# One buffer each for rounded q and its remainder, a 24th resident weight tile, fixed places for raw q and k, and GpSimd in order of need in the first pairs

## The chip, the cores and the metric

The kernel runs on one core of one Trainium2 chip. The metric is the device time of one execution in microseconds (us), which is a little longer than the span that the profile shows. Engines are named as in the profile: PE is TensorE, PEld its weight loads, DVE is VectorE, ACT is ScalarE, POOL is GpSimd, SP is SyncE, which here only issues transfers.

## What is computed

Causal attention for 8 batches of 12 heads (sequence 448, head size 64), and then a soft mixture of 8 experts with 4 slots each over the 3584 rows that come out:

```
scores = q @ k.T / sqrt(64), masked above the diagonal     # 96 heads, 448 x 448
attn   = softmax(scores);  x = attn @ v                    # x: 3584 x 768
logits = x @ phi                                           # 3584 x 32
d = softmax over rows of logits;   slot_input = d.T @ x    # 32 x 768
slot_out[e] = relu(slot_input[e] @ w1[e]) @ w2[e]          # w1: 768 x 1024, w2: 1024 x 768
c = softmax over slots of logits;  out = c @ slot_out      # 3584 x 768
```

## The kernel before

**Attention.** Two heads make a pair; there are 48 pairs, and `block(p)` (line 536) issues the work around pair p. Every engine runs its instructions in the order in which the program writes them (`_InOrder`, line 55). Transfers wait only for what they overwrite. Heads are numbered i = 2p and 2p + 1; the halves of a tile that hold them are h0 and h1.

Scores are exact sums of rounded parts. For each pair ACT rounds raw q into `qd` (`cast_q`, line 226) and raw k into `ks` (`cast_k`, line 230). The raw tiles hold the data twice, in partitions 0 to 63 and 64 to 127. POOL then puts the remainder of k into partitions 64 to 127 of `ks` (`sub_k`, line 234), and the remainder of q into partitions 64 to 127 of `r2` (`sub_q`, line 244). `copy_k2` (ACT, line 239) copies the rounded k beside a block of ones in `k2`. PE forms scores in two groups: `scores1` (line 250) multiplies `ks` by `qd`, and `scores2` (line 326) multiplies `k2` by `r2`. In between DVE finds maxima per row of the first group (`max_keys`, `max_row`), and POOL spreads their negatives into partitions 0 to 13 of `r2` (`max_spread`, line 315), so that `scores2` adds remainder and shift in one go. ACT takes the exponent (`exps`), and PE multiplies by v (`attv_pair`).

In block p, PE runs in this order: `scores2(2p)`, `scores1_all(2p+2)`, `scores2(2p+1)`, `scores1_all(2p+3)`, `attv_pair(p)` with a transposition of maxima in its middle, then logits work, transpositions, and on to the next block. POOL runs `sub_q(p+1)`, `sub_k(p+2)`, `max_spread(2p+2)`, `max_spread(2p+3)`. ACT runs `exps`, a copy, `exps`, `copy_k2(p+1)`, `cast_q(p+2)`, `cast_k(p+3)`. SP loads raw q for pair p+3 after `sub_q`, raw k for pair p+4 after `sub_k`, then v and in odd blocks a weight tile.

`scores1` of an even head above 4 reads two columns past its own half of `ks`, that is, the first two columns of the other head's half (`KP`, line 265).

`qd`, `ks` and `r2` have two buffers each, used by turns. Raw q and k share a pool of four buffers (line 92), and two early ones borrow room that weights take later.

**Experts.** The weights are 64 tiles of 128 x 1536 numbers (768 KB each), loaded in a fixed order by number n; six tiles per expert, w1 in four and the first half of w2 in two, then the second halves of w2. `RES` = 23 of them (n = 0 to 22) are loaded during attention into room of their own (`load_w`, line 163, called at line 542): the first 22 in pairs of tiles, the last alone in `wone`. `TW1` = 12 more (n = 23 to 34) go, one after the other, into the room that attention leaves (`wt[0]`, lines 822 to 824): each waits until the tiles that lay in its place were read for the last time. This room is taken from the raw tiles first, then `qd`, `ks`, `r2`, v and x, and the oldest tiles of the logits last. From n = 35 (which is loaded as part of a tile named `hw`) on, tiles go where a read weight tile lay, and in the resident room two at a time (1536 KB). SP issues all this in order.

The experts (`expert_in`, `expert_out`) run over e = 0 to 7; the last stage (`combine`) multiplies c by the slots' output and writes 11 MB out.

**The first pairs** have an order written out by hand (lines 505 to 531, and the cases for p == 0 in `block`). `warm` issues matmuls on no data of use; `START` and `WARM` are their numbers.

Of the kernel before, what the change touches and what calls it, by code (L numbers as in the profile page):

```python
# [9 lines left out]
F32 = mybir.dt.float32  # L10
F32R = mybir.dt.float32r
BF16 = mybir.dt.bfloat16
AF = mybir.ActivationFunctionType
# [4 lines left out]
P = 128  # L18
# [12 lines left out]
NEG = -float(2 ** 33)  # L31
NHD = 2 * NPAIR
NR, XB, XT = 2, 3, 2
RES, TW1 = 23, 12

HT = 2
WN, PAD = 1536, 168
WARM = (2, 5, 2, 3, 3)
START = (8, 3, 2)


FILL = 9
# [38 lines left out]
def attention_soft_moe(ctx: ExitStack, tc: tile.TileContext, qk, va, phi, w1, w2, out):  # L81
    nc = _Core(tc)
    const = ctx.enter_context(tc.tile_pool(name="const", bufs=1, side="left"))
    wone = ctx.enter_context(tc.tile_pool(name="wone", bufs=1, side="left"))
    wres = ctx.enter_context(tc.tile_pool(name="wres", bufs=RES // 2, side="left"))
    att, early = ExitStack(), ExitStack()

# [1 line left out]
    xtp = early.enter_context(tc.tile_pool(name="xtp", bufs=1, side="right"))  # L89
    wk = early.enter_context(tc.tile_pool(name="wk", bufs=1, side="right"))  # L90
    fix = early.enter_context(tc.tile_pool(name="fix", bufs=1, side="right"))
    raw = early.enter_context(tc.tile_pool(name="raw", bufs=4, side="right"))
    ps_1 = att.enter_context(tc.tile_pool(name="ps_1", bufs=1, space=PSUM))
    scs = ExitStack()
    ps_s = scs.enter_context(tc.tile_pool(name="ps_s", bufs=1, space=PSUM))
# [1 line left out]


    x_, va_, pt_ = [None] * XB, [None, None], [None, None]
    qd_, ks_ = [fix.tile([P, 2, S], F32R, name="qd0")], [fix.tile([P, 2 * S + KP], F32R, name="ks0")]  # L100
    r2_ = [fix.tile([P, 2, S], F32R, name="r20")]
    qd_.append(fix.tile([P, 2, S], F32R, name="qd1"))
    ks_.append(fix.tile([P, 2 * S + KP], F32R, name="ks1"))
    va_[0] = fix.tile([P, NCH, 2, VC], F32, name="va0")
    x_[1] = fix.tile([P, NCH, 3 * P], F32, name="x1")
    r_ = [fix.tile([P, RW], F32, name=f"r{i}") for i in range(2)]
    k2_ = fix.tile([P, 2 * S + KP], F32R, name="k2")
    r2_.append(fix.tile([P, 2, S], F32R, name="r21"))
    pt_[0] = wk.tile([P, 1024], F32, name="pt0")
    va_[1] = wk.tile([P, NCH, 2, VC], F32, name="va1")  # L110
    pt_[1] = wk.tile([P, 1024], F32, name="pt1")
# [10 lines left out]
    def load_qk(p, a, hs=slice(0, 2), eng=nc.sync):  # L122
        if p < NPAIR:
            if hs.start == 0:

                st["raw", a, p] = (wres.tile([P, 2 * WN], F32, tag="w", name=f"qk{a}_{p}")[:, 0:2 * S]
                                   .rearrange("p (h s) -> p h s", h=2)
                                   if (p, a) in ((1, 0), (2, 1)) else
                                   raw.tile([P, 2, S], F32, tag="qk", name=f"qk{a}_{p}"))
            eng.dma_start(out=st["raw", a, p][:, hs], in_=qk[p, :, a, hs])  # L130

    def loads_v(p, eng=nc.sync):
# [18 lines left out]
    def slot(n, name, dtype=F32):  # L151
        m = place(n)
        if m >= RES:
            return wt[0].tile([P, WN], dtype, tag=f"wa{m}", name=name)
        if m == RES - 1:
            return wone.tile([P, WN], dtype, tag="w1", name=name)
        k = (n - m, m // 2)
        if k not in twos:
            twos[k] = wres.tile([P, 2 * WN], F32, tag="w", name=name)
        t = twos[k][:, WN * (m % 2):WN * (m % 2) + WN]  # L160
        return t if dtype is F32 else t.bitcast(dtype)

    def load_w(n):
        if n < len(order):
            m, e, h, u = order[n]
            t = wtiles[order[n]] = slot(n, f"w{n}")
            src, q = (w1 if m == 0 else w2)[e, h], place(n)
            if n <= NBUF or q >= RES - 1:
                nc.sync.dma_start(out=t, in_=src[:, WN * u:WN * u + WN])
            elif u:  # L170

                nc.sync.dma_start(out=twos[n - q, q // 2], in_=src)
# [25 lines left out]
    for x in (x_[1], x_[0], x_[2]):  # L198
        nc.vector.memset(x[:, NCH - 1], 0.0)
    nc.scalar.activation(out=identb, in_=ident, func=AF.Copy)  # L200
    load_qk(1, 1, eng=nc.scalar)
    load_qk(2, 0)
    load_qk(3, 1)
    for i in range(NR):
        nc.gpsimd.memset(r2_[i][0:64, :, :].bitcast(F32), 0.0)
        nc.vector.memset(ks_[i][:, 2 * S:2 * S + KP].bitcast(F32), 0.0)
        nc.vector.memset(r_[i], -3.0e38)
    nc.vector.memset(k2_[0:64, 0:2 * S].bitcast(F32), 1.0)
# [5 lines left out]
    def warm(n, w=None, a=None):  # L214

        w = misc("warm") if w is None else w
        a, z = (identb, tri) if a is None else (a, a)
        for _ in range(n):
            nc.tensor.matmul(w, a, z.unsqueeze(1).to_broadcast([P, w.shape[1] // P, P]),
                             start=True, stop=True)  # L220
# [4 lines left out]

    def cast_q(p, hs=slice(0, 2)):
        if p < NPAIR:
            nc.scalar.activation(out=qd_[p % NR][:, hs], in_=st["raw", 0, p][:, hs], func=AF.Copy)

    def cast_k(p, hs=slice(0, 2)):  # L230
        if p < NPAIR:
            nc.scalar.activation(out=kv(p)[:, hs], in_=st["raw", 1, p][:, hs], func=AF.Copy)

    def sub_k(p, hs=slice(0, 2), eng=None):
        if p < NPAIR:
            ks = kv(p)[64:P, hs]
            (eng or nc.gpsimd).tensor_tensor(out=ks, in0=st["raw", 1, p][64:P, hs], in1=ks, op=ALU.subtract)
# [5 lines left out]

    def sub_q(p, hs=slice(0, 2), eng=None):
        if p < NPAIR:
            (eng or nc.gpsimd).tensor_tensor(out=r2_[p % NR][64:P, hs], in0=st["raw", 0, p][64:P, hs],
                                             in1=qd_[p % NR][64:P, hs], op=ALU.subtract)


    def scores1(i, part):  # L250
        if i >= NHD:
            return
        p, h = divmod(i, 2)
        ks, qd = ks_[p % NR], qd_[p % NR]
        if ("s", i) not in st:
            st["s", i] = s_[i % 3]
            st["open"] = set()
        s = st["s", i]

        bank = part in ("c12", "k1", "k2")  # L260
        start = bank not in st["open"]
        st["open"].add(bank)
        if part[0] == "k":
            c = int(part[1])
            o, w, m = S * h + P * c, S - CQ0[c], min(P, S - P * c + (KP if i > 4 or i % 2 else 0))
            nc.tensor.matmul(s[0:m, SCOL[c]:SCOL[c] + w], ks[:, o:o + m],
                             qd[:, h, CQ0[c]:S], start=start, stop=False, skip_group_check=True)
            return
        if part == "c12":
            o = s[:, SC1:SC1 + 2 * SC2].rearrange("p (a n) -> p a n", n=SC2)[:, :, 0:P]  # L270
            mask = tri.unsqueeze(1).to_broadcast([P, 2, P])
        else:
            o, mask = s[:, SC3:SC3 + AW + P], tri2
        nc.tensor.matmul(o, identb, mask, start=start, stop=False, skip_group_check=True)
# [40 lines left out]
    def max_spread(i):  # L315
        if i >= NHD:
            return
        p, h = divmod(i, 2)
        mr = st.pop(("mr", i))

        nc.gpsimd.affine_select(out=r2_[p % NR][0:NQB, h].rearrange("p (b t)->p b t", t=32),
                                in_=mr.unsqueeze(1).to_broadcast([NQB, NQB, 32]),
                                compare_op=ALU.is_equal, fill=0.0, base=0,
                                pattern=[[-1, NQB], [0, 32]], channel_multiplier=1)

    def scores2(i, cs):
        if i >= NHD:
            return
        p, h = divmod(i, 2)
        s = st["s", i]  # L330
        k2, r2 = k2_, r2_[p % NR]
        for c in cs:
            o, w, m = S * h + P * c, S - CQ0[c], min(P, S - P * c + (KP if i > 4 or i % 2 else 0))
            nc.tensor.matmul(s[0:m, SCOL[c]:SCOL[c] + w], k2[:, o:o + m],
                             r2[:, h, CQ0[c]:S], start=False, stop=True, skip_group_check=True)
# [169 lines left out]
    warm(START[0], a=x_[1][:, NCH - 1, 0:AW].bitcast(BF16))  # L505
    h0, h1 = slice(0, 1), slice(1, 2)
    cast_k(0, h0)
    cast_q(0, h0)
    copy_k2(0, h0)
    sub_k(0, h0, nc.vector)  # L510
# [8 lines left out]
    cast_k(0, h1)  # L519
    cast_q(0, h1)  # L520
    sub_k(0, h1)
    max_row(0, 0)
    max_row(0, 1)
    max_spread(0)
# [11 lines left out]
    def block(p):  # L536
        a, b = 2 * p, p // 6 - 1
        last, m6 = p == NPAIR - 1, p % 6
        if p + 1 < NPAIR:
            loads_v(p + 1, nc.sync if p + 1 < NPAIR - 1 else nc.scalar)  # L540
        if p % 2 and p // 2 < RES - 1 or p == 2 * RES - 2:
            load_w(p // 2)

        if last:
            for f in last_of:
# [5 lines left out]
        if p == 0:  # L551
            copy_k2(0, h1)
            cast_q(1, h1)
            max_row(1, 0)
            max_row(1, 1)
            max_spread(1)
            sub_k(1, h1, nc.vector)
        elif p > 1:
            xcopy(p - 2)
# [14 lines left out]
        if m6 == 2 and p > 6:  # L574
            logits_b(b)
        max_keys(a + 3, 0)
        if p:
            sub_q(p + 1)
            load_qk(p + 3, 0)
            sub_k(p + 2)  # L580
            load_qk(p + 4, 1)
        else:
            sub_q(1, h0)
            sub_k(2, h0)
        copy_k2(p + 1)
        if m6 == 2 and p > 6:
            logits_d(b, lt)
        cast_q(p + 2)
        cast_k(p + 3)
        if m6 == 3 and p > 6:  # L590
            logits_al(b)
        elif m6 == 4 and p > 6:
# [16 lines left out]
        attv_pair(p)  # L609
        max_row(a + 2, 1)  # L610
        max_spread(a + 2)
        if p == 0:
            sub_q(1, h1)
            load_qk(3, 0)
        for k in (1, 2):
            max_keys(a + 3, k)
        for k in range(2):
# [21 lines left out]
        if m6 == 2 and p > 6:  # L639
            logits_e(b, m, 1)  # L640
        max_spread(a + 3)
        if p == 0:
            sub_k(2, h1)
            load_qk(4, 1)
        if m6 in (1, 3, 5) and p > 1:
            logits_t(j, m[:, 0:P])
        for d, hf, sl, o in parts:
# [320 lines left out]
```

## Time and profile before

| | |
|---|---|
| median of 3 runs | 403.80 us (403.26 to 404.63) |
| profiled execution, its own time | 403.89 us |
| its span in the profile | 402.2 us |
| granted TensorE clock, mean | 0.984 |
| read from memory, written | 107.25 MB, 11.01 MB |

A profile row of the timeline gives start, duration, engine, operation, the tiles written and read, the shapes, and how many instructions were merged; in brackets stands idle time before it and what ended it. A row of the windows gives busy time of each engine in that stretch, the granted clock, the busy share of the 16 transfer engines and GB/s. A row of the chain of waits gives start, duration and the work that set the pace there.

### The profile page before, as it was taken

The page shows a single profiled execution, that of the slowest core. Times are in us where ns is not written, and L with a number is a line of the kernel's source. Part 1 is how long each engine was busy: PE and PEld are TensorE (multiplying, and loading weights), DVE is VectorE, ACT ScalarE, POOL GpSimd, SP SyncE. Part 2 cuts the span into 40 slices and gives each one's busy share as a digit, 9 for nine tenths or more (in the row PEclk, how much of TensorE's full clock was granted, in tenths as well). Part 3 has the DMA queues.
Part 4 walks back from the last instruction along what each step waited for, and adds up shares of the span by engine and source line. Part 5 has one row for each costly group of instructions (what it writes and reads, how often), then busy time and mean ns, then how long its engine had stood idle before and what let it go on. Part 6 is the DMA issues. An engine that isn't in the chain of part 4 may idle for free.

```text
span 402.2 us, 14066 instructions
## 1 busy us (share of the span) xinstructions
PE 368.3 (92%) x5756; PEld 295.8 (74%) x5756; DVE 293.7 (73%) x834; ACT 282.4 (70%) x395; POOL 265.3 (66%) x214
## 2 busy tenths in 40 slices
PE   6889899999999999999999999999999989997840
PEld 3678888898988898888888889888876544542420
DVE  5868788788898888898888888888975575342540
ACT  5878798898898888888888988988952112432430
POOL 5899899898898988898988989888950000000000
PEclk9999999999999999999999999999999999999985
DMA  8668877878787788777788787788679999999997
GB/s 304 230 199 282 271 266 228 245 279 278 229 286 262 244 269 289 256 240 265 262 270 259 249 272 238 274 286 257 216 279 415 420 420 423 424 418 413 398 397 339
DMA packets 34480, 119.17 MB, mean 296 GB/s; under 512 B 3824, under 2 KB 8944, under 8 KB 32880
## 3 DMA queue, kind: packets, MB, share of 16 engines
q1 hardware_dynamic: 34128, 117.55, 82.2%
q8 instruction: 45, 0.74, 0.7%
q10 hardware_dynamic: 288, 0.73, 0.5%
q14 instruction: 19, 0.16, 0.1%
HBM read 107.25 MB, written 11.01 MB: 294 GB/s over the span
## 4 chain that ended last, share of the span: by engine, by line
PE 54%; DMA 16%; POOL 12%; issue 5%; ACT 4%; DVE 4%; SPq 1%; POOLq 0%; DVEq 0%; ACTq 0%
PE s L65 28%; PE po L65 17%; DMA w<-in_w_dram 14%; POOL r L65 7%; POOL ks L65 5%; PE xm L65 3%; PE rt L65 1%; ACT ks L65 1%; PE pp L65 1%; DVE r L65 1%; DMA qk<-in_qk_dram 1%; PE hp L65 1%; ACT k L65 1%; DVE si L65 1%; PE e L65 1%
## 5 line engine op out<-in xcount | busy, mean ns | idle before, releaser
L65 DVE TRANSPOSE_TENSOR_REDUCE r<-s 128x32 f32<-128x1024 f32 x96 | 119.5, 1245 | 11.4 <-PE s L65 9.3
L65 ACT ACTIVATE pt<-s 128x1024 f32<-128x1024 f32 x96 | 98.8, 1029 | 40.6 <-PE s L65 37.8
L65 PEld LDWEIGHTS po<-va,pt 128*64 128x64 f32 x3040 | 103.6, 138 | 12.0 <-issue 11.9
L65 PE MATMUL po<-va,pt 128*64 128x65 f32 x3040 | 110.6, 224 | 0.0
L65 POOL TENSOR_TENSOR r<-qk,qd 64x896 fp32r<-64x896 f32 (+1 forms) x50 | 101.7, 2033 | 5.5 <-ACT qd L65 1.8
L65 POOL TENSOR_TENSOR ks<-qk,ks 64x896 fp32r<-64x896 f32 (+1 forms) x49 | 99.2, 2024 | 0.2
L65 PE MATMUL s<-qd,ks 128*128 128x448 f32 (+4 forms) x384 | 80.8, 322 | 0.6 <-POOL ks L65 0.4
L65 POOL TENSOR_SCALAR_AFFINE_SELECT r<-mr 14x448 fp32r<-14x448 f32 x96 | 61.5, 643 | 29.8 <-PE xm L65 18.6
L65 PE MATMUL s<-r,k 128*128 128x448 f32 (+3 forms) x384 | 65.2, 292 | 5.0 <-POOL r L65 4.3
L65 PEld LDWEIGHTS s<-r,k 128*128 128x128 f32 (+1 forms) x384 | 59.3, 176 | 11.0 <-POOL r L65 8.8
L65 PEld LDWEIGHTS s<-qd,ks 128*128 128x128 f32 (+2 forms) x384 | 52.8, 184 | 3.7 <-issue 1.4
L65 ACT ACTIVATE qd<-qk 128x896 fp32r<-128x896 f32 (+1 forms) x50 | 46.0, 920 | 1.7 <-DMA qk<-in_qk_dram 0.8
L65 ACT ACTIVATE k<-ks 64x896 fp32r<-64x896 f32 (+1 forms) x49 | 45.8, 934 | 1.2
L65 ACT ACTIVATE ks<-qk 128x896 fp32r<-128x896 f32 (+1 forms) x51 | 45.4, 892 | 1.1 <-DMA qk<-in_qk_dram 1.0
L65 PE MATMUL s<-tri,identb 128*128 128x192 bf16 x192 | 39.4, 270 | 1.1 <-DVE si L65 0.4
L65 DVE TENSOR_REDUCE r<-r 128x16 f32<-128x32 f32 x192 | 33.7, 176 | 5.0
L65 DVE TENSOR_REDUCE mr<-s 14x32 f32<-14x128 f32 x47 | 13.1, 279 | 23.1 <-ACT ks L65 12.8
L65 PE MATMUL xm<-ident,x 128*128 128x128 f32 x188 | 28.3, 273 | 0.0
L65 ACT ACTIVATE xts<-xm 128x512 f32<-128x512 f32 x47 | 27.8, 592 | 0.2 <-PE xm L65 0.2
L65 DVE TENSOR_SCALAR x<-po,sm 64x64 f32<-64x64 f32 x94 | 25.9, 276 | 0.7
L65 DVE TENSOR_TENSOR x<-po,sm 128x384 f32<-128x384 f32 (+2 forms) x49 | 25.7, 526 | 0.0
L65 DVE COPY ot<-pp 128x384 f32<-128x384 f32 x26 | 13.6, 554 | 13.4 <-PE pp L65 13.3
(138 smaller groups left out, 391.0 us busy)
## 6 DMA issues: line engine op xcount, KB each, us to landing
qk<-in_qk_dram SPq DMA_DIRECT2D x93, 448.0 KB, 4.4
w<-in_w_dram SPq DMA_DIRECT2D x43, 768.0 KB, 7.0
w<-in_w_dram SPq DMA_DIRECT2D x10, 1536.0 KB, 21.0
va<-in_va_dram SPq DMA_DIRECT2D x47, 260.0 KB, 4.6
out_dram<-ot SPq DMA_DIRECT2D x16, 384.0 KB, 6.7
out_dram<-ot SPq DMA_DIRECT2D x2, 1536.0 KB, 9.2
qk<-in_qk_dram SPq DMA_DIRECT2D x4, 224.0 KB, 3.9
hw<-in_w_dram SPq DMA_DIRECT2D x1, 768.0 KB, 8.4
```

The costliest lines, as they stand in the source:

```text
L65: return self._tc.keep_in_program_order(op(*args, **kwargs))
```

## The change

`qd` and `r2` have one buffer each. Raw q has two fixed places and raw k two, chosen by the pair's number. The 24th weight tile becomes resident, and the room that attention leaves takes 11 tiles instead of 12; the tile n = 22 is loaded in block 44 and n = 23 in block 45. In a block p above 1, POOL does `sub_k(p+2)` first and `sub_q(p+1)` second, and ACT `cast_k(p+3)` before `cast_q(p+2)`; in the blocks with p % 6 == 2 above 6, and in block 1, the second half of `sub_k(p+2)` comes after `max_spread(2p+2)`. In blocks 0 and 1 POOL's order changes, one clearing of `r2` goes, raw k of pair 1 is loaded by ACT later, and the numbers of `warm` matmuls change.

```diff
-RES, TW1 = 23, 12
+RES, TW1 = 24, 11
-START = (8, 3, 2)
+START = (9, 6, 2, 4)
...
-    raw = early.enter_context(tc.tile_pool(name="raw", bufs=4, side="right"))
...
-    qd_, ks_ = [fix.tile([P, 2, S], F32R, name="qd0")], [fix.tile([P, 2 * S + KP], F32R, name="ks0")]
-    r2_ = [fix.tile([P, 2, S], F32R, name="r20")]
-    qd_.append(fix.tile([P, 2, S], F32R, name="qd1"))
+    kraw = {n: fix.tile([P, 2, S], F32, name=f"kraw{n}") for n in (0, 1)}
+    qraw = {0: fix.tile([P, 2, S], F32, name="qraw0")}
+    ks_ = [fix.tile([P, 2 * S + KP], F32R, name="ks0")]
+    qraw[1] = fix.tile([P, 2, S], F32, name="qraw1")
+    qd = fix.tile([P, 2, S], F32R, name="qd")
     ks_.append(fix.tile([P, 2 * S + KP], F32R, name="ks1"))
...
-    r2_.append(fix.tile([P, 2, S], F32R, name="r21"))
+    r2 = fix.tile([P, 2, S], F32R, name="r2")
...
-                                   raw.tile([P, 2, S], F32, tag="qk", name=f"qk{a}_{p}"))
+                                   kraw[p % 2 if p > 1 else 1 - p] if a else qraw[p % 2 if p else 1])
...
-        if m == RES - 1:
-            return wone.tile([P, WN], dtype, tag="w1", name=name)
...
-            if n <= NBUF or q >= RES - 1:
+            if n <= NBUF or q >= RES:
...
-    load_qk(1, 1, eng=nc.scalar)
     load_qk(2, 0)
-    load_qk(3, 1)
+    nc.gpsimd.memset(r2[0:64, :, :].bitcast(F32), 0.0)
     for i in range(NR):
-        nc.gpsimd.memset(r2_[i][0:64, :, :].bitcast(F32), 0.0)
...
     cast_k(0, h0)
+    load_qk(1, 1, eng=nc.scalar)
     cast_q(0, h0)
...
-        if p % 2 and p // 2 < RES - 1 or p == 2 * RES - 2:
-            load_w(p // 2)
+        if p % 2 and p < 44 or p in (44, 45):
+            load_w(p // 2 + p // 45)
...
             cast_q(1, h1)
+            warm(START[3], pob)
...
-        if p:
+        late_k = p == 1 or m6 == 2 and p > 6
+        if p == 1:
+            sub_q(2, h0)
+            sub_k(3, h0)
+            sub_q(2, h1)
+            load_qk(4, 0)
+        elif p:
+            sub_k(p + 2, h0 if late_k else slice(0, 2))
+            if not late_k:
+                load_qk(p + 4, 1)
             sub_q(p + 1)
             load_qk(p + 3, 0)
-            sub_k(p + 2)
-            load_qk(p + 4, 1)
         else:
             sub_q(1, h0)
+            sub_q(1, h1)
+            load_qk(3, 0)
             sub_k(2, h0)
...
-        cast_q(p + 2)
-        cast_k(p + 3)
+        if p:
+            cast_k(p + 3)
+            cast_q(p + 2)
+        else:
+            cast_q(2)
+            cast_k(3)
...
         max_spread(a + 2)
-        if p == 0:
-            sub_q(1, h1)
-            load_qk(3, 0)
+        if p == 0 or late_k:
+            sub_k(p + 2, h1)
+            load_qk(p + 4, 1)
...
         max_spread(a + 3)
-        if p == 0:
-            sub_k(2, h1)
-            load_qk(4, 1)
```

More of the change, by code (lines that the diff above doesn't have):

```diff
@@ L83, in attention_soft_moe @@
     const = ctx.enter_context(tc.tile_pool(name="const", bufs=1, side="left"))
-    wone = ctx.enter_context(tc.tile_pool(name="wone", bufs=1, side="left"))
     wres = ctx.enter_context(tc.tile_pool(name="wres", bufs=RES // 2, side="left"))
@@ L227, in cast_q @@
         if p < NPAIR:
-            nc.scalar.activation(out=qd_[p % NR][:, hs], in_=st["raw", 0, p][:, hs], func=AF.Copy)
+            nc.scalar.activation(out=qd[:, hs], in_=st["raw", 0, p][:, hs], func=AF.Copy)
     def cast_k(p, hs=slice(0, 2)):
@@ L245, in sub_q @@
         if p < NPAIR:
-            (eng or nc.gpsimd).tensor_tensor(out=r2_[p % NR][64:P, hs], in0=st["raw", 0, p][64:P, hs],
-                                             in1=qd_[p % NR][64:P, hs], op=ALU.subtract)
+            (eng or nc.gpsimd).tensor_tensor(out=r2[64:P, hs], in0=st["raw", 0, p][64:P, hs],
+                                             in1=qd[64:P, hs], op=ALU.subtract)
     def scores1(i, part):
@@ L253, in scores1 @@
         p, h = divmod(i, 2)
-        ks, qd = ks_[p % NR], qd_[p % NR]
+        ks = ks_[p % NR]
         if ("s", i) not in st:
@@ L319, in max_spread @@
         mr = st.pop(("mr", i))
-        nc.gpsimd.affine_select(out=r2_[p % NR][0:NQB, h].rearrange("p (b t)->p b t", t=32),
+        nc.gpsimd.affine_select(out=r2[0:NQB, h].rearrange("p (b t)->p b t", t=32),
                                 in_=mr.unsqueeze(1).to_broadcast([NQB, NQB, 32]),
@@ L330, in scores2 @@
         s = st["s", i]
-        k2, r2 = k2_, r2_[p % NR]
+        k2 = k2_
         for c in cs:
@@ L521, in attention_soft_moe @@
     sub_k(0, h1)
+    load_qk(3, 1)
     max_row(0, 0)
```

## The prediction

> **What bounds the kernel now.** I read the page first: the share of each engine and the chain that ended last.
>
> ```profile
> PE 368.3 (92%) x5756; PEld 295.8 (74%) x5756; DVE 293.7 (73%) x834; ACT 282.4 (70%) x395; POOL 265.3 (66%) x214
> ...
> PE 54%; DMA 16%; POOL 12%; issue 5%; ACT 4%; DVE 4%; SPq 1%; POOLq 0%; DVEq 0%; ACTq 0%
> ```
>
> PE carries half the chain and transfers 16%; that is an average over two stages. The chain in order of time says where they change places, and the windows what transfers do there.
>
> ```profile
> 317.06 12.56 DMA w<-in_w_dram
> 329.68 29.73 DMA w<-in_w_dram
> 359.47 15.03 DMA w<-in_w_dram
> 374.54 0.85 PE so L65 x8
> ```
>
> ```profile
> 288.00:292.00 4.00, 4.00 (x100) 3.62 (x98) 3.53 (x9) 3.77 (x6) 3.93 (x3) 1.00 0.05 16
> 298.00:360.00 62.00, 58.05 (x817) 32.85 (x811) 33.67 (x116) 17.08 (x45) 2.28 (x9) 1.00 1.01 419
> 374.00:400.00 26.00, 10.85 (x46) 6.68 (x46) 8.69 (x18) 7.15 (x16) 0.00 (x0) 0.79 1.04 404
> ```
>
> From 317 to 374.5 weights set the time, and from 374 to 400 the output does: the transfer engines are full (share 1.01 and 1.04) from 298 on without a break. Just before, from 288 to 292, they are empty (0.05), while PE is full. So there are two prices: before 298 a microsecond counts if PE or what PE waits for loses it; after 298 only bytes count, and how early they can start. One tile is 768 KB, 0.786 MB; at 419 GB/s that is 1.87 us.
>
> **The change part by part: the end.** What moves is seen on POOL's and SP's rows in blocks 45 and 46, the last that hold subtractions.
>
> ```profile
> 287.13 2.11 POOL L65 TENSOR_TENSOR r<-qk,qd 64x896 fp32r<-64x896 f32 x1
> 289.19 2.12 POOL L65 TENSOR_TENSOR ks<-qk,ks 64x896 fp32r<-64x896 f32 x1
> 291.38 0.64 POOL L65 TENSOR_SCALAR_AFFINE_SELECT r<-mr 14x448 fp32r<-14x448 f32 x1
> 292.94 0.64 POOL L65 TENSOR_SCALAR_AFFINE_SELECT r<-mr 14x448 fp32r<-14x448 f32 x1 [0.92 <-PE xm L65]
> 293.66 2.11 POOL L65 TENSOR_TENSOR r<-qk,qd 64x896 fp32r<-64x896 f32 x1
> ```
>
> ```profile
> 295.79 0.33 SPq L65 DMA_DIRECT2D w<-in_w_dram  x1
> ```
>
> ```profile
> 310.31 0.98 SPq L65 DMA_DIRECT2D w<-in_w_dram  x2
> 313.85 0.33 SPq L65 DMA_DIRECT2D hw<-in_w_dram  x1
> ```
>
> ```profile
> hw<-in_w_dram SPq DMA_DIRECT2D x1, 768.0 KB, 8.4
> ```
>
> Before, tile 23 waits for `sub_k(47)` (done at 291.31) and tile 24 for `sub_q(47)` (293.66 + 2.11 = 295.77; issued at 295.79), since their places hold raw tiles. From there the queue holds tiles 24 to 35, twelve of them, and the last (`hw`) lands at 313.85 + 8.4 = 322.25. That is 295.79 + 12 x 1.87 = 318.2 and 4.0 more for start and completion.
>
> After, tile 23 has room of its own and is issued in block 45, into the empty stretch from 288: it costs nothing, being covered by PE's work there; without that stretch it would cost its 1.87. Counting bytes (3584 per raw place, 6144 per weight tile), tile 24 needs the two k places, tile 25 a k place, a q place and `ks0`, tile 26 the last q place. `sub_k(47)` now goes first, so tile 24 starts at about 289.3 to 290, tile 25 after `sub_q(46)`, at about 292; both land before 297. Tile 26 waits for `sub_q(47)`, which now also waits for `scores2(93)` to have read the only `r2`:
>
> ```profile
> 294.07 0.62 PE L65 MATMUL s<-r,k 128*128 128x448 f32 x4
> ```
>
> so 294.7 + 2.1 = 296.9. Then ten tiles, 26 to 35: 296.9 + 10 x 1.87 + 4.0 = 319.6, against 322.25: 2.6 us earlier. The queue must not run dry meanwhile. `hw` is gated by PE at 313.85; a tile alone takes 4.5 to land, so it can't land before 318.35.
>
> ```profile
> DMA to landing us min/median/max: 4.5/7.4/10.1
> ```
>
> 319.6 is 1.3 later, so the gate does not bind yet; 318.35 bounds the gain at 3.9. If tiles 24 and 25 gained nothing, the one resident tile would be left: 1.9. I take 2.5, a tenth off for a short gap when tile 33 (issued at 310.31) comes. All behind it, weights and output, is a full queue and moves with it. Singles fall by two and loads of two tiles rise by one, equal bytes.
>
> **Part two: the pairs.** For an ordinary pair the order on POOL turns round, but the two operations are as long as each other, so `max_spread` starts when it did. The rows of pairs 14 and 15:
>
> ```profile
> 98.87 2.11 POOL L65 TENSOR_TENSOR r<-qk,qd 64x896 fp32r<-64x896 f32 x1
> 100.93 2.10 POOL L65 TENSOR_TENSOR ks<-qk,ks 64x896 fp32r<-64x896 f32 x1
> 103.10 1.28 POOL L65 TENSOR_SCALAR_AFFINE_SELECT r<-mr 14x448 fp32r<-14x448 f32 x2
> 104.46 2.11 POOL L65 TENSOR_TENSOR r<-qk,qd 64x896 fp32r<-64x896 f32 x1
> 106.53 2.10 POOL L65 TENSOR_TENSOR ks<-qk,ks 64x896 fp32r<-64x896 f32 x1
> 108.70 0.64 POOL L65 TENSOR_SCALAR_AFFINE_SELECT r<-mr 14x448 fp32r<-14x448 f32 x1
> ```
>
> ```profile
> 105.09 0.37 PE L65 MATMUL s<-r,k 128*128 128x448 f32 x1
> ```
>
> ```profile
> 108.86 0.93 ACT L65 ACTIVATE ks<-qk 128x896 fp32r<-128x896 f32 x1
> ```
>
> New waits in pair 15: `sub_q(16)` for `scores2(31)`, which runs from 105.09 and is done by 105.8, while POOL comes to it at 106.53; and `cast_q(17)` for `sub_q(16)`, done at 108.63, while ACT comes to it at 108.86. Behind `cast_q` ACT has the next exponent and PE the next `scores1`, at 109.96 + 0.6 = 110.6; `cast_q` is done at 109.8. So these pairs cost nothing; the cover is 0.2 us on ACT and 0.8 on PE. Raw k is loaded 2 us earlier, raw q 2 us later; the transfers and SP, which waits behind neither, have that room.
>
> The seven pairs with p % 6 == 2 (8, 14, ..., 44) do cost. Before, in pair 14, the maxima were there at 102.29 + 0.24, but POOL was busy until 103.03. Now `sub_k` is cut in two halves of 1.14 (row below, 14.50), one of them behind `max_spread(30)`:
>
> ```profile
> 102.29 0.24 DVE L65 TENSOR_REDUCE mr<-rt 14x32 f32<-14x128 f32 x1
> ```
>
> ```profile
> 104.41 0.25 PE L65 MATMUL s<-qd,ks 128*66 128x64 f32 x1
> ```
>
> ```profile
> 109.96 0.45 PE L65 MATMUL s<-r,k 128*128 128x448 f32 x1
> ```
>
> `max_spread(30)` 102.57 to 103.21, second half of `sub_k` 103.28 to 104.42, `max_spread(31)` 104.5 to 105.14. PE can start pair 15 some 0.3 us sooner, but its first `scores1` reads two columns of the other head (66 in the row at 104.41), so it waits for that second half: 104.45 instead of 104.41. The gain is gone. Then `scores2(31)` at 105.17 instead of 105.09, and POOL, which ends its spreads 0.75 later, brings pair 16 to 109.96 + 0.15. PE is full afterwards and can't make it good. Bounds per pair: -0.3 (the wait goes and nothing follows) and +0.3; I take +0.15, by these rows. Seven of them: +1.05.
>
> **Part three: the first pairs.** POOL sets the pace up to pair 3.
>
> ```profile
> 13.40 1.14 POOL L65 TENSOR_TENSOR r<-qk,qd 64x448 fp32r<-64x448 f32 x1
> 14.50 1.14 POOL L65 TENSOR_TENSOR ks<-qk,ks 64x448 fp32r<-64x448 f32 x1
> 16.41 0.64 POOL L65 TENSOR_SCALAR_AFFINE_SELECT r<-mr 14x448 fp32r<-14x448 f32 x1 [0.76 <-DVE mr L65]
> ```
>
> ```profile
> 29.96 1.43 POOL L65 TENSOR_SCALAR_AFFINE_SELECT r<-mr 14x448 fp32r<-14x448 f32 x2
> ```
>
> The new order fills the 0.76 of idle time at 16.41 but cuts two more operations in halves (two times 1.14 for 2.10) and adds pauses between. Laid out from 13.40 with these durations, the spread of 29.96 starts at 29.8: -0.2; later pairs start from there.
>
> ```profile
> 1.39 3.59 PE L65 MATMUL warm<-x 128*128 128x512 bf16 x8 [1.39 <-DVE x L65]
> 4.78 0.37 PE L65 MATMUL s<-tri,identb 128*128 128x192 bf16 x1
> 5.37 0.32 PE L65 MATMUL s<-qd,ks 128*64 128x64 f32 x1 [0.23 <-ACT qd L65]
> ```
>
> The later load of raw k of pair 1 lets raw q of pair 0 land sooner (ACT waits for it before 5.37), but a ninth `warm` takes 0.45 (3.59 / 8) from 4.78, which is all of that. The other `warm` matmuls lie where PE waits for maxima, and the clearing saved on POOL (before 5) where it waits for data. Bounds -0.7 and +0.2; I take -0.15. Together -0.35.
>
> **Sum.** -2.5 + 1.05 - 0.35 = -1.8. From the profiled execution's 403.89 that is 402.1; this execution lies 0.09 above the median of 403.80, so 402.0.
>
> **A rule against it.** The Trainium skill (Trainium Kernel Development and Optimization, Best Practices) advises two buffers, so that transfers overlap with computation; here two buffers become one for `qd` and `r2`. The trace does not bear a cost out for ordinary pairs, because the one use of each buffer ends before its next filling comes up in the order. Read strictly, that rule leads to the second rival's time.
>
> **Rivals.**
> 1. The late pairs cost nothing, and the first pairs give more (-0.7, the bound above, and -0.2). For it: POOL is idle a little in nearly every pair (0.92 at 292.94), so 0.15 may be made good. Against: PE is full in between. 403.8 - 2.5 - 0.9 = 400.4.
> 2. Slower: the single buffers stall. Place: `cast_q` behind `sub_q` on ACT, and the exponent behind it. The cover is 0.2 us; if POOL comes 0.3 later than I reckon, ACT is late by 0.1 in each of about 40 pairs, +4.0: 402.0 + 4.0 = 406.0. It decides from 1.8 / 40 = 0.045 per pair. Against: PE has 0.8 to spare at the same place.
> 3. The queue runs dry: tiles 24 and 25 go no sooner, or tiles 33 to 35 come late, and only 1 us of the end's gain is left: 403.8 - 1.0 + 0.7 = 403.5. For it: the margin is 1.3 us.
> 4. The tile does not do what it should: with the transfers at the end set by PE's releases, nothing is gained, and the pairs' cost stays: 403.8 + 0.7 = 404.5. Against: the share of 1.01 from 298.
>
> **How the numbers follow.** A measurement of this kernel tells 0.3%, 1.2 us, from no change: faster is below 402.6. My forecast has 0.47 (its own range 401.2 to 403.0, so 0.36 of it faster and 0.11 the same), rival 1 0.20 (faster), rival 2 0.10 (slower), rival 3 0.14 and rival 4 0.09 (the same). Faster 0.56, same 0.34, slower 0.10. The range from 400.4 to 404.5 takes in the four cases on the near side and leaves out the slower one and half of the first rival.
>
> **What would show it.** Tile 23 lands before 290 and the transfers are busy between 288 and 297; `hw` lands near 319.7; weights end near 372 against 374.5. In pairs 15, 21 and so on, PE waits for POOL's `ks` before `scores1`. In ordinary pairs ACT does not wait for POOL. The prediction is wrong if ACT waits for `r` in most pairs, if the wait for `ks` is much over 0.3, or if the share of transfers falls below 1 between 298 and 320.

## The result, and the profile after

| | before | after |
|---|---|---|
| median of 20 runs | 404.73 us (403.02 to 407.40) | 407.05 us (405.32 to 408.96) |
| profiled execution, its span | 403.89, 402.2 us | 408.50, 406.8 us |
| granted TensorE clock in it | 0.984 | 0.975 |

The changed kernel is slower: the ratio is 1.006, 95% interval 1.0042 to 1.0078, some 2.4 us. (Medians leave out one run of e8 further down, 583.77 us at a granted clock of 0.558.) The two profiled executions lie 4.6 apart, because that of before is 0.84 under its median and that of after 1.45 over its own. So the traces tell where time went, and the medians how much it is on average.

Chain of waits of the kernel after: shares by engine (the chain can be followed back only to 297.97 us, so they add up to 23%), then its two longest pieces in order of time:

```profile
DMA 12%; PE 8%; ACT 1%; issue 1%; DVE 1%; DVEq 0%; SPq 0%
```

```profile
331.13 29.20 DMA w<-in_w_dram
...
360.39 18.64 DMA w<-in_w_dram
```

The last weights land at 360.39 + 18.64 = 379.03, against 374.50 before (359.47 + 15.03). The windows that answer to those of the prediction:

```profile
288.00:292.00 4.00, 3.85 (x80) 3.50 (x79) 3.72 (x14) 3.95 (x7) 3.36 (x4) 1.00 0.96 353
298.00:360.00 62.00, 58.13 (x863) 35.01 (x865) 35.89 (x123) 19.21 (x47) 5.09 (x11) 1.00 0.99 396
374.00:400.00 26.00, 14.09 (x74) 8.02 (x66) 9.91 (x21) 8.16 (x18) 0.00 (x0) 0.87 1.04 400
```

The stretch from 288 to 292 is no longer empty (0.96 for 0.05), as it should be. But from 298 to 360 the transfers move 396 GB/s where it was 419. Part of this is only that everything comes some 5 us later: from 303 to 365 they move 408. What is missing lies at its beginning, 380 GB/s from 303 to 325 for 413 from 298 to 320 before. How late things come is seen on the first exponent of pair 8 and of pair 47, on ACT, before:

```profile
61.81 1.03 ACT L65 ACTIVATE pt<-s 128x1024 f32<-128x1024 f32 x1 [0.70 <-PE s L65]
```

```profile
300.14 1.02 ACT L65 ACTIVATE pt<-s 128x1024 f32<-128x1024 f32 x1 [2.79 <-issue]
```

and after:

```profile
64.90 1.03 ACT L65 ACTIVATE pt<-s 128x1024 f32<-128x1024 f32 x1 [0.68 <-PE s L65]
```

```profile
305.16 1.02 ACT L65 ACTIVATE pt<-s 128x1024 f32<-128x1024 f32 x1 [2.85 <-issue]
```

PE's work of pair 8 is 3.09 us late already, that of pair 47 is 5.02 late. Of this, the end gives back 5.02 - 4.53 = 0.49. "Lateness" below is this difference of exponent rows against the kernel before, in one profiled execution of each. Three things are to be explained: +3.1 in the first pairs, +1.9 over the attention, and a gain of 0.5 at the end where 2.5 was forecast.

**First pairs.** ACT's rows up to the first exponent, before:

```profile
1.41 0.37 ACTq L65 DMA_DIRECT2D qk<-in_qk_dram  x1
...
7.09 1.03 ACT L65 ACTIVATE ks<-qk 128x448 fp32r<-128x448 f32 x2
...
10.85 1.02 ACT L65 ACTIVATE pt<-s 128x1024 f32<-128x1024 f32 x1 [2.26 <-PE s L65]
```

after:

```profile
3.44 0.38 ACTq L65 DMA_DIRECT2D kraw<-in_qk_dram  x1
...
10.72 1.04 ACT L65 ACTIVATE ks<-kraw 128x448 fp32r<-128x448 f32 x2 [3.67 <-DMA kraw<-in_qk_dram]
11.67 0.56 ACT L65 ACTIVATE qd<-qk 128x448 fp32r<-128x448 f32 x1
12.13 1.00 ACT L65 ACTIVATE pt<-s 128x1024 f32<-128x1024 f32 x1
```

Raw k of pair 1 goes out 2 us later (3.44 for 1.41) but is there 3.6 us later: its cast is at 10.72 for 7.09, after 3.67 of waiting. Its landing takes 7.3 us. The transfer queues between 3.5 and 6.5 us, before (total, SP's queue, ACT's queue):

```profile
DMA packets 550, 1.20 MB, mean 400 GB/s; under 512 B 64, under 2 KB 366, under 8 KB 550
...
q1 hardware_dynamic: 409, 0.75, 65.7%
q10 hardware_dynamic: 141, 0.45, 37.3%
```

after:

```profile
DMA packets 392, 0.80 MB, mean 266 GB/s; under 512 B 41, under 2 KB 288, under 8 KB 392
...
q1 hardware_dynamic: 392, 0.80, 89.5%
```

Before, ACT's queue brought nearly all of raw k of pair 1 (0.45 MB) in this stretch, beside 0.75 MB of SP's. After, not one packet of ACT's queue moves, and SP's queue alone moves 0.80 MB: 266 GB/s for 400. Then PE waits 1.80 us for this k, and 0.91 for POOL behind it:

```profile
12.56 0.25 PE L65 MATMUL s<-qd,ks 128*64 128x64 f32 x1 [1.80 <-POOL ks L65]
```

And the granted clock (third column from the right) falls:

```profile
14.00:16.00 2.00, 1.24 (x6) 1.20 (x6) 1.04 (x3) 1.04 (x2) 1.78 (x2) 0.57 0.49 123
16.00:18.00 2.00, 2.00 (x20) 1.56 (x21) 0.58 (x1) 1.96 (x3) 1.87 (x2) 0.50 0.85 333
```

**Late pairs.** Lateness is flat at 3.26 to 3.28 from pair 11 to pair 14, then 2.88, 3.51, 3.60 at pairs 15, 16, 17, and flat again; so in each of the seven pairs with p % 6 == 2 above 6, 0.28 on average (1.93 / 7). POOL in pairs 14 to 16, after:

```profile
106.58 1.15 POOL L65 TENSOR_TENSOR ks<-kraw,ks 64x448 fp32r<-64x448 f32 x1
...
108.51 2.11 POOL L65 TENSOR_TENSOR ks<-kraw,ks 64x896 fp32r<-64x896 f32 x1
110.58 2.11 POOL L65 TENSOR_TENSOR r<-qraw,qd 64x896 fp32r<-64x896 f32 x1
112.75 0.64 POOL L65 TENSOR_SCALAR_AFFINE_SELECT r<-mr 14x448 fp32r<-14x448 f32 x1
```

and PE:

```profile
107.78 0.25 PE L65 MATMUL s<-qd,ks 128*66 128x64 f32 x1 [0.16 <-POOL ks L65]
...
113.45 0.73 PE L65 MATMUL s<-r,k 128*128 128x448 f32 x4
```

The second half of `sub_k(16)` (106.58) stands between the two spreads. PE's first `scores1` of the odd head waits 0.16 for it, as forecast. The second spread then ends at 107.79 + 0.64 = 108.43; less the lateness of 3.26 that was there before pair 14, this is 105.17, for 103.10 + 1.28 = 104.38 in the kernel before: 0.79 later. POOL ends `sub_q(16)` at 112.69, and `scores2(32)` follows its spread at 113.45, which is 109.96 + 3.49, so the lateness has grown by 0.23.

### The profile page after: what moved, and what is told of

Read it like the earlier page. It is cut to its first block, busy times and chain, and to the rows that moved or that the text cites. A ratio compares the mean times of both kernels' runs of the same rounds, so it can differ in the third digit from the quotient of the medians.

```text
span 406.8 us, 14062 instructions
## 1 busy us (share of the span) xinstructions
PE 372.4 (92%) x5764; PEld 298.2 (73%) x5764; DVE 294.7 (72%) x834; ACT 286.8 (71%) x395; POOL 266.7 (66%) x222
## 5 line engine op out<-in xcount | busy, mean ns | idle before, releaser
L65 PEld LDWEIGHTS po<-va,pt 128*64 128x64 f32 x3040 | 105.4, 139 | 11.8 <-issue 11.4
L65 PE MATMUL po<-va,pt 128*64 128x65 f32 x3040 | 112.5, 225 | 0.0
L65 POOL TENSOR_TENSOR ks<-kraw,ks 64x896 fp32r<-64x896 f32 (+1 forms) x55 | 98.8, 1796 | 7.3 <-ACT ks L65 3.1
L65 POOL TENSOR_TENSOR r<-qraw,qd 64x896 fp32r<-64x896 f32 (+1 forms) x49 | 99.7, 2036 | 3.3 <-ACT qd L65 1.8
L65 PE MATMUL s<-r,k 128*128 128x448 f32 (+3 forms) x384 | 66.3, 295 | 3.7 <-POOL r L65 3.7
L65 ACT ACTIVATE ks<-kraw 128x896 fp32r<-128x896 f32 (+1 forms) x49 | 44.9, 919 | 7.4 <-DMA kraw<-in_qk_dram 5.9
L65 ACT ACTIVATE qd<-qraw 128x896 fp32r<-128x896 f32 (+1 forms) x48 | 44.8, 933 | 6.8 <-POOL r L65 4.8
L65 PE MATMUL s<-tri,identb 128*128 128x192 bf16 x192 | 40.5, 269 | 1.5 <-DVE si L65 0.3
```

Source lines behind the costliest of these rows:

```text
L65: return self._tc.keep_in_program_order(op(*args, **kwargs))
```

## The experiments

Each kernel was compared with the kernel before on the same chip; ratios are to that. A difference of two ratios is good to about 1 us. "Lateness" is at pair 8 and at pair 47.

| kernel | median, us | before, us | ratio, 95% interval | lateness |
|---|---|---|---|---|
| after | 407.05 | 404.73 | 1.0060 (1.0042 to 1.0078) | +3.09, +5.02 |
| e1 | 407.07 | 404.03 | 1.0078 (1.0064 to 1.0091) | +1.74, +4.18 |
| e2 | 404.54 | 404.03 | 1.0010 (0.9994 to 1.0026) | +2.10, +2.09 |
| e3 | 406.89 | 404.03 | 1.0066 (1.0049 to 1.0082) | +1.89, +3.77 |
| e5 | 406.24 | 404.67 | 1.0026 (1.0003 to 1.0050) | +1.92, +4.07 |
| e6 | 405.09 | 404.67 | 1.0003 (0.9981 to 1.0025) | -0.22, +2.05 |
| e7 | 407.55 | 404.67 | 1.0067 (1.0046 to 1.0088) | +1.92, +1.90 |
| e8 | 403.90 | 404.67 | 0.9981 (0.9960 to 1.0002) | +1.45, +1.40 |
| e9 | 402.49 | 404.39 | 0.9955 (0.9938 to 0.9973) | -0.56, -0.69 |
| e10 | 403.18 | 404.39 | 0.9966 (0.9953 to 0.9979) | -0.30, -0.44 |
| e11 | 405.81 | 404.39 | 1.0041 (1.0027 to 1.0054) | -0.23, +2.23 |
| e12 | 401.68 | 404.68 | 0.9923 (0.9897 to 0.9949) | at pair 47 -0.72 |
| e13 | 397.57 | 404.68 | 0.9819 (0.9791 to 0.9846) | at pair 47 -0.30 |

### e1: raw k of pair 1 issued before the first cast

```diff
     cast_k(0, h0)
-    load_qk(1, 1, eng=nc.scalar)
...
     nc.scalar.activation(out=identb, in_=ident, func=AF.Copy)
+    load_qk(1, 1, eng=nc.scalar)
     load_qk(2, 0)
```

> The changed kernel with one DMA issue put back: raw k of pair 1 is issued on ACT's queue before the first cast, as in the kernel before, instead of behind it. Theory: the late load is what made the start 3.1 us longer in the profiled run (ACT waits 3.67 us for it, PE 1.80, and PE's granted clock then falls to half from 14.4 to 21.2), so the load lands near 8 again, the first exponent of pair 9 comes at or before its time in the kernel before (was 2.7 later), and the median falls from 407.05 by 1.5 to 3.4: 403.6 to 405.5, 404.6 taken. Rival 1: the start is slow by the new order on GpSimd (the spreads and halves of pairs 0 to 3), and the load is only where the wait shows: the median stays at 406.5 to 407.5. Rival 2: the early load takes the transfers from q of pair 0 and gives back what it saves; then the first scores of pair 0 come 0.7 later and the gain is under 1: 406.

ACT's rows:

```profile
3.45 0.40 ACTq L65 DMA_DIRECT2D kraw<-in_qk_dram  x1
...
10.21 1.04 ACT L65 ACTIVATE ks<-kraw 128x448 fp32r<-128x448 f32 x2 [2.18 <-DMA kraw<-in_qk_dram]
```

The edit did not do what it says: the issue stayed at 3.45, about when the first k is there (in the kernel after, the cast that waits for it starts at 3.43). Why the issue waits, although it overwrites nothing that is in use, is not shown. The time stayed too, which is the first rival's number, but says nothing for its reason. This tells only that the place in the program is not enough; e5 and e6 put the question again.

### e2: the late pairs' subtraction whole

```diff
-        late_k = p == 1 or m6 == 2 and p > 6
+        late_k = p == 1
```

> The changed kernel with the subtraction of k whole in the seven late pairs (p % 6 == 2, p > 6); pair 1 stays cut in halves. Theory: each of the seven costs 0.28 us on PE in the profile of the changed kernel, and PE's lateness passes to the end in full: 7 x 0.28 = 1.9 less, median 405.1; the lateness against the kernel before no longer steps up at pairs 10, 16, 22. Rival: the halves only exchange a wait for another (before, the spread of these pairs waited 0.5 for the whole subtraction), so each step stays within 0.1 and the median at 406.4 to 407.2.

Lateness is +2.10 at pair 8 and +2.09 at pair 47: no step is left, in 39 pairs. The median is 0.5% under that of the kernel after (1.0010 for 1.0060), 2.0 us for the 1.9 expected. So the cut halves are the whole of the loss from pair 8 on, and the single buffers of `qd` and `r2` and the turned order cost ordinary pairs nothing.

### e3: PE kept busy while it waits for k

```diff
-START = (9, 6, 2, 4)
+START = (9, 6, 6, 4)
...
+        if p == 0:
+            warm(7, pob)
         scores1_all(a + 2)
```

> The changed kernel with eleven more 128x512 warm matmuls in the first block: seven behind the first two rows of maxima, where PE waits 1.80 us for k of pair 1, four more behind scores1 of pair 1, where it waits 0.91. The late load stays. Theory: PE's idle time makes the granted clock fall to half from 14.4 to 21.2 us, and this is some 1.5 of the 3.1 us; with PE busy the clock stays at 1.0, the first exponent of pair 1 comes at 20.4 to 20.8 instead of 22.07, and the median falls by 0.5 to 1.5: 406. Rival: the clock falls whatever PE does there, or the wait for the load (1.8) is all of it: 407, and 407.3 if the warm matmuls hold PE up.

In this profile the clock stays at 1.0 and lateness at pair 8 is 1.89 for 3.09. e2, which waits as the kernel after does, also kept its clock in its profile and has 2.10. So the fall cost the profiled execution after about 1.0 to 1.2 us, and the late load itself about 2. The median did not fall (1.0066), and the rival's 407 is nearer. That fits with a shorter fall, or none, in most runs of the kernel after: the profiled one has a mean clock of 0.975, and 15 of the 20 have 0.980 or more, as the profiled executions of e1 and e7 have, with falls half as long. Where the clock fell in the other runs is not shown.

### e5: the same load first of all on ACT's queue

```diff
+    load_qk(1, 1, eng=nc.scalar)
     nc.scalar.activation(out=identb, in_=ident, func=AF.Copy)
...
     cast_k(0, h0)
-    load_qk(1, 1, eng=nc.scalar)
```

> The changed kernel with raw k of pair 1 issued on ACT's queue as ACT's first instruction of all, so that it waits for nothing (in e1 it still waited for the first k to land and went out at 3.45). Theory: the load's place costs the start 2.1 us (without the fall of the clock), because k comes at 10.2 to 11.6 instead of 7.1, and because from 3 to 5.5 us SP's queue alone moves its small transfers at 160 to 280 GB/s, where both queues together moved 380 to 435. So k lands by 7.5, the transfers are over 380 GB/s from 3.5 on, the lateness at pair 8 falls from 2.1 to between -0.3 and +0.5, and the median is 1.6 to 2.4 under that of the changed kernel (taken as 406.5 beside a kernel before of 404.0): 404.5. Rival: the order on GpSimd and the one qd in the first block are the cost (its sub_q of pair 1 waits for scores2, and the cast of pair 1 waits for sub_q), and the lateness at pair 8 stays over 1.2: 405.8.

```profile
4.80 0.58 ACT L65 ACTIVATE ks<-kraw 128x448 fp32r<-128x448 f32 x1 [1.96 <-DMA kraw<-in_qk_dram]
```

Now k of pair 1 is there in time (its cast at 8.01), but it takes the transfers from k of pair 0: the first cast is at 4.80 for 3.43, and all that follows is 1.6 late. Lateness is 1.92, near the 2 us of the late load, but from another load. The time is nearer the rival's 405.8, but its reason is not here: POOL and the one `qd` are as in e6, which has no such cost. It is the trade that the second rival of e1 named.

### e6: the same load on SP's queue, fifth

```diff
         load_qk(0, 0, hs)
+    load_qk(1, 1)
     load_qk(1, 0)
...
     cast_k(0, h0)
-    load_qk(1, 1, eng=nc.scalar)
```

> The changed kernel with raw k of pair 1 issued on SP's queue, fifth, before raw q of pair 1. Theory of the two queues: it no longer waits behind q1, v0, k2 and q2, but one queue alone moves these transfers at 160 to 280 GB/s, so k lands at 8 to 9, and the lateness at pair 8 is 0.5 to 1.3: median 405.2, between the changed kernel and e5. Rival: only the place in the order counts; then it does as well as e5 or better, since ACT issues one transfer less (0.4 us).

```profile
9.30 1.04 ACT L65 ACTIVATE ks<-kraw 128x448 fp32r<-128x448 f32 x2 [1.92 <-DMA kraw<-in_qk_dram]
...
10.98 1.01 ACT L65 ACTIVATE pt<-s 128x1024 f32<-128x1024 f32 x1
```

k is there at 9.3, a little past the 8 to 9 of the theory of the two queues, and the first pairs are 0.22 ahead of the kernel before, where the theory had them 0.5 to 1.3 late; the outcome is the rival's. There is slack: before, ACT waited 2.26 us for PE ahead of the first exponent (row 10.85). A cast of k at 9.30 is inside it, one at 10.72 is not. Against the kernel after, 1.0003 for 1.0060: 2.3 us, the cost of the load's place.

### e7: the kernel before with the load late

```diff
     nc.scalar.activation(out=identb, in_=ident, func=AF.Copy)
-    load_qk(1, 1, eng=nc.scalar)
-    load_qk(2, 0)
-    load_qk(3, 1)
...
     cast_k(0, h0)
+    load_qk(1, 1, eng=nc.scalar)
+    load_qk(2, 0)
+    load_qk(3, 1)
```

> The kernel before with the issue of raw k of pair 1 (and of raw q of pair 2 and raw k of pair 3, that follow it) moved behind the first cast, as the changed kernel has it. Theory: this alone makes k land at 9.5 to 11 and costs 1 to 2 us: lateness at pair 8 between 1.0 and 2.0, median 405.0 to 406.0 beside 404.0. Rival, that the start is slow by GpSimd's new order and the single buffers: within 0.5 of the kernel before.

The two further loads move along because the kernel before with raw k of pair 1 alone moved (e4, expected 1.5 to 3.4 us over the kernel before) deadlocks and has no time. SP issues them in the same row as before, from 3.61 on.

```profile
10.45 1.04 ACT L65 ACTIVATE ks<-qk 128x448 fp32r<-128x448 f32 x2 [1.86 <-DMA qk<-in_qk_dram]
```

```profile
12.00:14.00 2.00, 1.71 (x7) 0.69 (x7) 1.41 (x3) 1.95 (x4) 1.93 (x3) 0.72 0.51 182
```

Nothing else of the change is in it, and it is as slow as the whole change: 1.0067, lateness 1.92 from pair 8 to the end, and the clock falls here as well (0.72). The rival is refuted: the cost is there without GpSimd's new order and the single buffers. The median, 2.9 over before (2.7 by ratio), is more than the 2.0 expected at most; the fall of the clock was not in that reckoning.

### e8 and e9: both repairs

e8 is e5 and e2 together, e9 is e6 and e2.

> e5 and e2 together: raw k of pair 1 first on ACT's queue, and the subtraction of k whole in the seven late pairs. Theory: both costs are gone and the gain of the end is left: PE's chain at the end of the attention within 0.5 of the kernel before, the end 1.0 to 1.5 earlier against PE, median 402.0 to 403.2 beside 404.0 (ratio 0.995 to 0.998). Rival, that the end is set by PE's releases and the 24th tile brings nothing: 404.0.

> e6 and e2 together: raw k of pair 1 fifth on SP's queue, and the subtraction of k whole in the seven late pairs. Theory: the first pairs are then 0.2 us ahead of the kernel before and stay so to the end of the attention (lateness -0.3 to 0.0), and the end gains 0.8 to 1.4 against PE, so 1.0 to 1.6 under the kernel before: ratio 0.996 to 0.9975. By the prediction's price of the end, 2.5, it would be 2.7 under (0.993); if the tile brought nothing, 0.2 under (0.9995).

e9 is faster than both kernels: 402.49 us, 1.8 under before (1.9 by medians) and 4.2 under after by ratio. Its attention ends 0.69 ahead, more than the 0.3 of its theory, and its weights end at 373.03 (the chain's last piece: 354.32 + 18.71), 1.47 ahead: the end gains 0.8, the least that the theory gave it. The 0.993 by the prediction's price of the end and the 0.9995 of a tile that brings nothing both lie outside the interval. e8 keeps 1.4 us of lateness from e5's start, where 0.5 was forecast, and is 1.0 over e9 by ratio.

### e10: e9 without the 24th tile

```diff
-RES, TW1 = 24, 11
+RES, TW1 = 23, 12
...
+        if m == RES - 1:
+            return wone.tile([P, WN], dtype, tag="w1", name=name)
```

> e9 with 23 resident tiles and 12 behind them, loaded as in the kernel before; everything else is e9, so the difference from e9 is the price of the 24th tile. Theory: a transfer is gained, but the tiles from 28 on wait for what PE releases at a spacing near their own 1.87 us, so the tile is worth 0.5 to 1.2: the median is that much over e9. The prediction's sum for the end: 2.5 over e9 (1.9 for the tile by itself). Fourth rival of the prediction: no difference. In the trace, hw is issued at the same time against PE in both, and lands 7.3 after its issue in e9 and 8 to 8.5 after it here.

It is 0.69 us slower by medians and 0.0011 by ratio (0.45 us; the intervals overlap), far from 1.9 or 2.5. But this does not price the tile. SP's issues from tile 23 on, e9:

```profile
285.90 24.69 SPq L65 DMA_DIRECT2D w<-in_w_dram  x12
```

and here:

```profile
285.71 0.38 SPq L65 DMA_DIRECT2D va<-in_va_dram  x1
286.15 24.70 SPq L65 DMA_DIRECT2D w<-in_w_dram  x12
```

Without the resident place, tile 23 still goes out right behind the issue ahead of it and waits for nothing, and all twelve keep the rhythm of e9, 0.25 later, as PE is at pair 47. Probably the two buffers given up (2 x 3584 bytes) leave room for a tile (6144 bytes) that nothing else holds. So e10 shows that the tile's being resident changes no issue; what the room by itself is worth, no run here shows. `hw` was to land 8 to 8.5 after its issue here and took 7.1, for 7.2 in e9: this theory had the place wrong.

### e11: two columns more in the first part

```diff
-            sub_k(p + 2, h0 if late_k else slice(0, 2))
+            sub_k2(p + 2, 0, S + KP) if late_k else sub_k(p + 2)
...
-            sub_k(p + 2, h1)
+            sub_k2(p + 2, S + KP, 2 * S) if p > 1 else sub_k(p + 2, h1)
```

Made on e6; `sub_k2` is `sub_k` on columns a to z of both halves taken as one row.

> e6 with the cut of the late pairs' subtraction two columns further right: the first part takes 450 of the 896 columns and so holds the two that scores1 of the other head reads. Theory 1, the prediction's mechanism: scores1 of the odd head waits for the second part only through these columns (0.43 us on PEld in pair 14), and without them the cost of 0.28 per pair falls under 0.1: lateness at the end of the attention 2.05 - 1.4 = 0.6, median 1.0 to 1.4 under e6. Theory 2: POOL sets it, since the second part stands ahead of the second spread and both spreads end later; then the 0.28 stays, and the median is that of e6.

PE in pairs 15 and 16, e6:

```profile
104.44 0.25 PE L65 MATMUL s<-qd,ks 128*66 128x64 f32 x1
...
110.11 0.74 PE L65 MATMUL s<-r,k 128*128 128x448 f32 x4
```

and here:

```profile
104.22 0.25 PE L65 MATMUL s<-qd,ks 128*66 128x64 f32 x1
...
110.13 0.73 PE L65 MATMUL s<-r,k 128*128 128x448 f32 x4
```

The first `scores1` of the odd head starts 0.22 sooner and no longer waits for POOL's `ks`, and `scores2(32)` is at 110.13 for 110.11; lateness still grows to 2.23. The wait that the prediction named is real and costs nothing; POOL sets the pace. That the kernel is 0.7 us over e6 by medians (1.5 by ratio) is not explained; 0.18 of it is lateness at pair 47.

### e12 and e13: half tiles where releases gate, and where they don't

```diff
+    HALF = {order[n] for n in range(29, 35)}      # e12; range(42, 48) in e13
...
-                nc.sync.dma_start(out=t, in_=src[:, WN * u:WN * u + WN])
+                z = WN // 2 if order[n] in HALF else WN
+                nc.sync.dma_start(out=t[:, 0:z], in_=src[:, WN * u:WN * u + z])
```

(Loads of two tiles and the experts' reads likewise.)

> e9 with only half of each of the six tiles 29 to 34 loaded (the experts take the loaded half twice, so PE's work is the same, and the output is another): 2.36 MB less, 5.6 us of a full queue at 419 GB/s. These six and hw are issued between 300.4 and 313.2, each when attention's end gives its room back, at a spacing of 1.8 us, which is about their own transfer time. Theory: here the releases set the pace. hw can't go out sooner, and a lone tile takes 4.5 to land, so hw lands 2.7 sooner at most and the end comes 2.0 to 2.8 earlier than in e9: median 399.7 to 400.5 beside 402.5. Rival, the prediction's picture of a full queue from 298 on: bytes alone count, 5.6 earlier: 396.9.

> e9 with half of each of the six tiles 42 to 47 (three loads of two tiles), the same bytes left out further back in the queue, where ten loads lie ahead of the transfers; the experts take the loaded half twice, as in e12, and the output is another. Theory: here only bytes count, so the end comes 5.0 to 5.8 earlier than in e9: median 396.7 to 397.5. If PE's releases set the pace all along the tail, it is no more than in e12.

The same 2.36 MB left out gain 1.3 us in e12 (0.9955 - 0.9923; the intervals overlap) and 5.5 in e13 (0.9955 - 0.9819). Weight issues of e9, tiles 29 to `hw`:

```profile
300.40 0.33 SPq L65 DMA_DIRECT2D w<-in_w_dram  x1
...
303.49 1.43 SPq L65 DMA_DIRECT2D w<-in_w_dram  x2
...
307.10 0.33 SPq L65 DMA_DIRECT2D w<-in_w_dram  x1
...
309.61 0.98 SPq L65 DMA_DIRECT2D w<-in_w_dram  x2
...
313.15 0.33 SPq L65 DMA_DIRECT2D hw<-in_w_dram  x1
```

Seven tiles go out from 300.40 to 313.15, six intervals in 12.75 us, so one each 2.1 us (not the 1.8 that was expected), each when attention's end gives room; a tile takes 1.87. The releases are slower than the transfers. In windows, last columns share and GB/s, before:

```profile
302.00:308.00 6.00, 5.37 (x106) 4.29 (x99) 2.87 (x13) 1.55 (x3) 0.00 (x0) 1.00 1.01 407
308.00:314.00 6.00, 5.88 (x92) 3.93 (x93) 2.87 (x13) 1.45 (x6) 0.00 (x0) 1.00 1.02 417
```

e9:

```profile
302.00:308.00 6.00, 5.32 (x98) 4.09 (x97) 2.76 (x13) 1.53 (x4) 0.00 (x0) 1.00 1.02 350
308.00:314.00 6.00, 5.93 (x102) 4.04 (x102) 2.69 (x12) 0.90 (x4) 0.00 (x0) 1.00 1.00 394
```

e12 and e13:

```profile
308.00:314.00 6.00, 5.93 (x103) 4.04 (x102) 2.67 (x12) 0.90 (x4) 0.00 (x0) 1.00 0.72 194
```

```profile
308.00:314.00 6.00, 5.88 (x97) 3.97 (x99) 2.83 (x12) 1.23 (x6) 0.00 (x0) 1.00 1.01 386
```

With half tiles behind the gates the transfers stand idle (0.72, 194 GB/s): the releases set the pace there. Further back the bytes do. In e9 the share stays near 1 while the rate falls to 350 and 394 GB/s; there the rate tells, not the share. e12 gained less than the 2.0 expected: `hw` landed 6.0 after its issue, not 4.5.

```profile
hw<-in_w_dram SPq DMA_DIRECT2D x1, 768.0 KB, 6.0
```

## Why the prediction was wrong, point by point

**First pairs (forecast -0.35): the step that failed most.** The prediction wrote that "the later load of raw k of pair 1 lets raw q of pair 0 land sooner" and priced only that. It did not ask when k itself would land, nor what it now stands behind: all but one of the transfers that SP had issued before it (last section). k came 3.6 us later, past the 2.26 us of slack that stood in the trace of before. Price: 2.3 us by e6, and 2.7 in e7, where nothing else of the change is made. What was reckoned of POOL's order and `warm` is borne out as far as one execution of each can: with the load repaired the first pairs are 0.19 (e13) to 0.62 (e12) ahead, where 0.35 was forecast.

**Ordinary pairs (forecast 0): right.** e2's lateness is flat, +2.10 at pair 8 and +2.09 at pair 47. The second rival, stalls of the single buffers, is refuted. The Trainium skill (Trainium Kernel Development and Optimization, Best Practices) would have two buffers; in these pairs the one buffer's use ends before its refill comes up, as argued.

**Late pairs (forecast +0.15 each, bounds -0.3 to +0.3): the term was mis-sized.** It is +0.28, 1.93 instead of 1.05 in sum. The mechanism behind the forecast's number, POOL that "ends its spreads 0.75 later", was right (0.79 in pair 14), the wait for the two columns beside the point (e11). What is left of it on PE came to 0.28, not 0.15.

**End (forecast -2.5): mis-sized.** `sub_q(47)` ended when forecast: tile 26 went out at 301.99 in the kernel after, 296.97 on the clock of before, for 296.9. The step that failed is "The queue must not run dry meanwhile": only `hw`'s own gate was tested. Tiles 29 to 34 have gates too, 2.1 us apart, so an early start finds no more to carry. From 284 to 302 us e9 moves 5.33 MB where before it was 4.41, a lead of 0.92 MB or 2.2 us of a full queue; from 302 to 314 it moves 4.46 where it was 4.94, and 0.48 MB or 1.1 us of the lead is gone. In the kernel after:

```profile
hw<-in_w_dram SPq DMA_DIRECT2D x1, 768.0 KB, 7.3
```

1.1 us less than the 8.4 of before is all that `hw` gained, and its issue is no earlier against PE (318.87 - 5.02 = 313.85). Against PE the weights end 0.5 (after) to 0.8 (e9) sooner, 0.2 in e10. The 1.9 for the one resident tile is shown by no run. The time is near the third rival's 1.0, by its late tiles 33 to 35, and the mechanism is the fourth's, releases; the chance of 0.14 was too small, since the rows (the issues from 301 to 313.85) were in the trace. The sign that the prediction set itself, a share below 1 between 298 and 320, came: 0.94 for 1.02 before, though 0.99 when the stretch is moved by the lateness.

**Sum.** Forecast -2.5 + 1.05 - 0.35 = -1.8. Measured, by ratios: start +2.3 (e6), late pairs +2.0 (e2), the rest of the change -1.8 (e9), together +2.5, each good to about 1 us; the kernel after has +2.4. No rival was slower for the right reason: the one that ended slower was the stall that did not come.

## What to carry to other kernels

A transfer that is issued later is late by more than its delay, if other transfers get in front of it: before moving a load, find its first reader, the slack there, and what stands in the queue between. More room helps an ordered stream of loads only up to the next load that waits for a release; list all gates to come and compare their spacing with the transfer time of one load. Before a run that leaves out one part is read as the price of that part, look at the issue times: in e1 and e10 what was meant to move did not. An instruction cut in two to let something by pays on the engine that runs it, and if that engine paces the next stage, all of that beyond its cover is lost.

## What the runs showed of the hardware

SP's queue alone moved 266 GB/s between 3.5 and 6.5 us in the kernel after; with ACT's queue beside it, it was 400 before. This is no limit of one queue with small packets: before, from 5 to 6.5 us, SP's queue alone moved 397 GB/s, 246 of its 305 packets under 2 KB. What held it to 266 is not shown. And ACT's queue was not served at once: no packet in the 3 us behind its issue. Its first packet came by 6.8 us, when SP's queue had moved 1.36 MB, near the 1.38 of the first five transfers, issued up to 2.66; before, it came by 3.5 us, when SP's had moved 0.38, near the 0.46 of the first two. So a transfer on the second queue stood, in effect, behind most of what the first queue had been given before it. The transfer's row before (issue to landing in the last column):

```profile
qk<-in_qk_dram ACTq DMA_DIRECT2D x1, 448.0 KB, 4.0
```

and after:

```profile
kraw<-in_qk_dram ACTq DMA_DIRECT2D x1, 448.0 KB, 7.3
```

The Trainium skill (DMA: Bandwidth & Descriptors, Queues, rings and completion order) states that each engine takes turns between queues packet by packet. While both move, the trace agrees: 0.42 MB of SP's and 0.35 of ACT's from 7 to 9 us. By that rule alone k, once moving, would be through after twice its 0.46 MB, some 2.4 us at the 380 GB/s that moved from 7 to 10 us, an estimate; 141 of its 144 packets were through at 10.0, 3.2 us after the first. Why there was no turn for it in the 3 us before is not shown.

The granted clock went back to half after waits of only 1.80 and 0.91 us in the first block, and stayed there for 6.8 us, worked out from the rows of 2 us (14 to 16: 0.57, then 0.50, 0.50 and 0.73); in e1 and e7 it was 3.4 us each. e2 had the same waits (1.82 and 0.92), and its clock stayed at 1.00. The Trainium skill (TensorE: Matmul & The Clock Gate, Part 1) says that the clock has two levels and is set by how busy PE was over free-running windows of about 3.4 us, so that it varies from run to run; the levels of 0.50 and 1.00, the lengths of 3.4 and twice 3.4 us, and e2 agree. It has the half clock follow an idle window; here no single wait was that long, and the fall came all the same.
